# Loading two weight matrices in fp32 on SyncE's queue and casting them on POOL, in a kernel of channel attention and gelu

## The chip, the cores and the metric

The kernel runs on one core of a Trainium2 chip. The metric is the time of one execution in device microseconds (us). The granted clock is the share of the full TensorE clock in the profile's record. Engines are called by the names of the profile: PE (TensorE), DVE (VectorE), ACT (ScalarE), POOL (GpSimd), SP (SyncE). SP's loads stand in the profile as the hardware queue, POOL's as the software queue. A load lands when its last byte has arrived; a casting load turns fp32 into bf16 on its way.

## The reference

```python
B, N, C = 4, 6080, 256                                    # q, k, v: fp32
qn = q / (norm(q, axis=1) + 1e-06); kn = k / (norm(k, axis=1) + 1e-06)
s  = kn.transpose(0, 2, 1) @ qn / tau                     # 256 x 256 for each batch
a  = softmax(s)                                           # over the last axis
x  = (v @ a).reshape(24320, 256)
h  = x @ w_in                                             # w_in 256 x 2048
g  = gelu_tanh(h)
out = g @ w_out                                           # w_out 2048 x 256
```

## The kernel before

The kernel multiplies the attention of each batch into w_in (`aw`), so that the main loop has two stages for each block of 512 tokens: hp = v·aw with gelu on ACT, and yp = g·w_out. For the first batch, q and k come in fp32 on SP's queue in eight chunks, into a ring of four staging buffers, and the products q·k and the column sums must be complete before anything else can start; this opening takes some 41 us. The next batches' attention is woven into the main loop.

The parts that matter here: the four staging buffers, the small copy that holds POOL back until chunk 5 has landed, and the casting loads of the weights on POOL's queue.

```python
stage = ctx.enter_context(tc.tile_pool(name="stage", bufs=4))
# ... for each chunk n of the first batch: cast on DVE, square on ACT, products on PE, then
        for x in ((2, 3) if n == 0 else (4, 5) if n == 1 else (n + 4,)):
            stage_chunk(x)                                # next loads on SP's queue
        if n == n_chunks - 3:
            nc.gpsimd.tensor_copy(gate[:, 0:1], st[1][0:1, 0, 0:1])
# ... v block 0 in fp32 on SP's queue, then
    for c0, c1 in ((0, 1024), (1024, D)):
        nc.gpsimd.dma_start(out=win_bf[:, :, c0:c1], in_=win_v[:, :, c0:c1])
    load_v(1)
    for half in range(2):
        nc.gpsimd.dma_start(out=wout_bf[:, half * 8 : half * 8 + 8, :],
                            in_=wout_v[:, half * 8 : half * 8 + 8, :])
    load_v(2)
# ... norms, Gs, its transposes T, eT = exp(T); then the first products with w_in (first_aw),
#     aw scaled on DVE and ACT, and the main loop:
    #   hp  L584: lhsT=aw,  rhs=vT       yp  L510: lhsT=g, rhs=wout_bf[:, fc, :]
    #   in the first block, yp of fc 0-3, 4-7 and 8-11 follow hp groups 5, 6 and 7
```

Of the kernel before, what the change touches and what calls it, by code (L numbers as in the profile page):

```python
# [8 lines left out]
FP32 = mybir.dt.float32  # L9
# [9 lines left out]
def kernel(  # L19
# [10 lines left out]
    nc = tc.nc  # L30
    B, N, C = q.shape
    D = moe_w_in.shape[1]
# [12 lines left out]
    stage = ctx.enter_context(tc.tile_pool(name="stage", bufs=4))  # L45
# [19 lines left out]
    SMAX = 6  # L65
# [22 lines left out]
    def slots_of(chunk, rest=REM):  # L88
        _, size, rem = chunk
        return [(s, 128) for s in range(size)] + ([(size, rest)] if rem else [])  # L90
# [9 lines left out]
    def halves(pool, tag, dtype, size, most=SMAX):  # L100

        tiles = [pool.tile([128, 2, most, 256], dtype, tag=tag, name=tag)
                 for _ in range(1 if size <= most else 2)]
        if len(tiles) == 1:
            return [tiles[0][:, x] for x in range(2)], tiles[0]
        return [t.rearrange("p a b c -> p (a b) c") for t in tiles], None

    def stage_chunk(n):
        if n < len(first_chunks):
            _, size, rem = first_chunks[n]  # L110
            if n < SHARED:
                st, whole = halves(stage, "st", FP32, size)
            else:

                _, size, rem = first_chunks[n - 2]
                whole = staged[n - 2][1][:, :, size + rem :, :]
                st = [whole[:, x] for x in range(2)]
                rem = False

            if rem:  # L120
                nc.gpsimd.memset(whole[:, :, size, :], 0.0)
            load_chunk((nc.sync, nc.scalar if n < 1 else nc.sync), st, 0, first_chunks[n], 2)
            staged.append((st, whole))
# [16 lines left out]
    gate = const.tile([1, 8], FP32)  # L140
# [3 lines left out]
    win_bf = const.tile([128, 2, D], BF16)  # L144
    wout_bf = const.tile([128, FC, 256], BF16)
    win_v = moe_w_in.rearrange("(c p) d -> p c d", p=128)
    wout_v = moe_w_out.rearrange("(t p) d -> p t d", p=128)

    def keep_clock(n, pool=pH, tag="h"):

        for _ in range(n):
            idle = pool.tile([128, 2, 512] if pool is pH else [128, 512], FP32, tag=tag, name="idle")
            nc.tensor.matmul(idle[:, 0, :] if pool is pH else idle, lhsT=filler[:, 0:128], rhs=filler, start=True, stop=True)

    def gram(G, qk, s, rows, first, last):
        for ic in range(2):
            nc.tensor.matmul(  # L157
                G[:, ic, :],
                lhsT=qk[1][:rows, s, ic * 128 : ic * 128 + 128],
                rhs=qk[0][:rows, s, :],  # L160
                start=first and ic == 0,
                stop=last,
                skip_group_check=True,
            )
# [66 lines left out]
    n_chunks = len(first_chunks)  # L231
    seen, summed = 0, 0

    def sums_of(parts, last):
        nonlocal summed
        for m, x in enumerate(parts):
            col_sums(cols, x, ones_bf[: x[0].shape[0], :], summed == 0, last and m == len(parts) - 1)
            summed += 1

    def pairs_of(n, sqb):  # L240

        size = first_chunks[n][1]
        h = size // 2
        pair, whole = halves(prp, "pair", BF16, h, SMAX // 2)
        for x in range(2):
            nc.vector.tensor_add(pair[x][:, 0:h], sqb[x][:, 0:h], sqb[x][:, h : 2 * h])
        parts = [[y[:, s, :] for y in pair] for s in range(h)]
        if size % 2:
            parts.append([y[:, size - 1, :] for y in sqb])
        if first_chunks[n][2]:  # L250
            parts.append([y[:, size, :] for y in sqb])
        sums_of(parts, False)

    waiting = None
    for n, ch in enumerate(first_chunks):
        st, whole = staged[n]
        size = ch[1]
        qkb, qk_whole = halves(qkp, "qk", BF16, size)
        sqb, sq_whole = halves(sqp, "sq", BF16, size)
        hi = size + ch[2]  # L260
        if whole is None:
            todo = list(zip(qkb, sqb, st))
        else:
            todo = [[y[:, :, 0:hi] for y in (qk_whole, sq_whole, whole)]]
        for to, sq, x in todo:
            nc.vector.tensor_copy(to, x)  # L266
            if n != n_chunks - 2:
                nc.scalar.activation(sq, x, AF.Square)  # L268
        if n == n_chunks - 2:
            nc.scalar.activation(sqb[1][:, 0:hi], st[1][:, 0:hi], AF.Square)  # L270
            nc.vector.tensor_mul(sqb[0][:, 0:hi], qkb[0][:, 0:hi], qkb[0][:, 0:hi])
        keep_clock(fillers[n])
        for s, rows in slots_of(ch, 128):
            gram(G, qkb, s, rows, seen == 0, seen == n_all - 1)
            seen += 1
        if waiting is not None:
            pairs_of(*waiting)
            waiting = None
        if n < 2:
            pairs_of(n, sqb)  # L280
        elif n < TAIL:
            waiting = (n, sqb)
        else:
            sums_of([[y[:rows, s, :] for y in sqb] for s, rows in slots_of(ch, 128)], n == n_chunks - 1)

        for x in ((2, 3) if n == 0 else (4, 5) if n == 1 else (n + 4,)):
            stage_chunk(x)
        if n == n_chunks - 3:
            nc.gpsimd.tensor_copy(gate[:, 0:1], st[1][0:1, 0, 0:1])

    v0 = stage.tile([128, 2, SMAX, 256], FP32, tag="st", name="v0")
    v0 = v0.rearrange("p a b c -> p (a b) c")[:, 0:4, :]
# [2 lines left out]
    def v_parts(nb):  # L295
        blk = nb % n_blocks
        cols = min(BLK, N - blk * BLK)
        return (nb // n_blocks) * N + blk * BLK, cols // 128, cols % 128
# [4 lines left out]
    def load_v(nb):  # L303
        if nb >= B * n_blocks:
            return
        r0, n, rest = v_parts(nb)
        t = vin.tile([128, 4, 256], BF16, tag="v", name="vb")
        nc.gpsimd.dma_start(  # L308
            out=t[:, 0:n, :],
            in_=v_rows[r0 : r0 + n * 128, :].rearrange("(p s) c -> p s c", s=n))  # L310
        if rest:
            nc.gpsimd.dma_start(out=t[:rest, n, :], in_=v_rows[r0 + n * 128 : r0 + n * 128 + rest, :])
        v_of[nb] = t
# [27 lines left out]
            load_chunk((nc.gpsimd, nc.gpsimd), views, b, later_chunks[n])  # L341
            loaded_of[b, n] = views, t

    for c0, c1 in ((0, 1024), (1024, D)):
        nc.gpsimd.dma_start(out=win_bf[:, :, c0:c1], in_=win_v[:, :, c0:c1])
    load_v(1)
    for half in range(2):
        nc.gpsimd.dma_start(out=wout_bf[:, half * 8 : half * 8 + 8, :],
                            in_=wout_v[:, half * 8 : half * 8 + 8, :])
    load_v(2)  # L350


    r = smx.tile([128, 4], FP32, tag="r", name="r")
# [5 lines left out]
    for cc in range(2):  # L359
        p = pH.tile([128, 2, 512], FP32, tag="h", name="vps")[:, 0, :]  # L360
# [183 lines left out]
    for b in range(B):  # L544
# [5 lines left out]
        for blk in range(n_blocks):  # L550
# [27 lines left out]
            for i in range(NP):  # L578
# [12 lines left out]
                if before is not None:  # L591
                    n = -(-len(before["todo"]) // (NP - i))
                elif i >= NP - 3:

                    n = 4
                else:
                    n = 0
# [58 lines left out]
```

## Time and profile before

| | value |
|---|---|
| time | 756.42 us, median of 3 (756.24 to 757.38) |
| span in the profile | 754.2 us, granted clock 1.0 |
| PE busy | 733.3 us, 97% |
| first gelu matmul (hp) | 41.05 us |
| first half of w_in landed | 39.61 us |

The two lines that say most are from the view of waits of PE (engine and line, what it waited for; total us, times, longest). The view has four rows. Apart from PE's wait for the first casts of q and k (15.6 us, 14.4 of them before its first instruction), the first row here is the only one above half a microsecond, and the only one that a load of weights causes:

```profile
PE ps L384 <- DMA win_bf<-in_moe_w_in_dram: 1.3, 1, 1.3
PE T L195 <- DVE Gs L187: 0.3, 1, 0.3
```

The profile's time at which a matmul group starts is what I compare below. Since the opening takes a few tenths of a microsecond more or less from one execution to the next, I count from the transposes of v block 0, which stand right after the last product of the opening: they start at 35.86, the first gelu matmul follows 5.19 us later, and the second block's first gelu matmul (52.32) 16.46 us later.

### The profile page before, as it was taken

How to read it: one execution, taken by the hardware profiler on the slowest of the kernel's cores; microseconds unless marked ns; L12 is line 12 of the kernel's file. 1: busy time of each engine (PE TensorE's matmuls, PEld its weight loads, DVE VectorE, ACT ScalarE, POOL GpSimd, SP SyncE). 2: the span in 40 equal slices, each digit the busy share in tenths (PEclk: the TensorE clock that was granted, in tenths of full speed). 3: DMA queues.
4: the chain of work that ended last, by engine and by line, in shares of the span. 5: the costliest groups of instructions: out<-in, count | busy, mean ns of one | idle time of the engine just before them, and what ended most of it. 6: DMA issues, size and time to landing. Idle time of an engine off the chain costs nothing.

```text
span 754.2 us, 12371 instructions
## 1 busy us (share of the span) xinstructions
PE 733.3 (97%) x5262; PEld 503.5 (67%) x5262; DVE 277.5 (37%) x485; ACT 420.3 (56%) x411; POOL 75.6 (10%) x150
## 2 busy tenths in 40 slices
PE   2999999999999999999999999999999999999998
PEld 1656666776666666776666666766767666666666
DVE  3733556454401546554521265555441011011011
ACT  4875555555456555555555555555546655555552
POOL 1311111101012102101001102010101000000000
PEclk9999999999999999999999999999999999999999
DMA  9999685615147685813435776661513543322111
GB/s 368 346 190 156 103 150 137 118 43 83 48 93 143 114 161 108 162 52 60 99 57 118 140 117 121 148 133 46 83 43 80 96 95 74 69 74 54 41 56 57
DMA packets 79639, 83.59 MB, mean 111 GB/s; under 512 B 55392, under 2 KB 59104, under 8 KB 79072
## 3 DMA queue, kind: packets, MB, share of 16 engines
q0 software_dynamic: 17104, 32.97, 27.4%
q1 hardware_dynamic: 62176, 48.20, 23.8%
q10 hardware_dynamic: 304, 1.64, 0.5%
q8 instruction: 41, 0.67, 0.4%
q14 instruction: 14, 0.11, 0.0%
HBM read 78.91 MB, written 24.90 MB: 138 GB/s over the span
## 4 chain that ended last, share of the span: by engine, by line
PE 94%; DMA 4%; ACT 1%; issue 0%; DVE 0%; SPq 0%; POOL 0%; DVEq 0%
PE yp L510 44%; PE hp L584 44%; PE G L157 4%; PE ps L217 2%; ACT sq L268 1%; DMA st<-in_q_dram 1%; DMA st<-in_k_dram 1%; DMA win_bf<-in_moe_w_in_dram 1%; PE cols L169 0%; PE yp L615 0%; PE T L195 0%; DVE aw L404 0%; PE vps L422 0%; PE ps L384 0%; PE rs L204 0%
## 5 line engine op out<-in xcount | busy, mean ns | idle before, releaser
L588 ACT ACTIVATE g<-hp 128x1024 bf16<-128x1024 f32 (+1 forms) x384 | 389.8, 1015 | 308.2 <-PE hp L584 308.2
L510 PE MATMUL yp<-wout_bf,g 128*128 128x256 bf16 x3024 | 392.0, 273 | 0.0
L584 PE MATMUL hp<-vT,aw 128*128 128x512 bf16 (+1 forms) x1536 | 390.8, 377 | 0.2 <-DVE aw L404 0.2
L510 PEld LDWEIGHTS <-g 128*128 128x128 bf16 x3024 | 295.9, 98 | 113.4
L584 PEld LDWEIGHTS <-aw 128*128 128x128 bf16 x1536 | 149.9, 98 | 104.7 <-issue 0.6
L527 DVE COPY ysb<-yp 128x512 f32<-128x512 f32 (+1 forms) x95 | 64.9, 683 | 402.5 <-PE yp L510 402.5
L451 DVE TENSOR_TENSOR acc<-acc,sq 128x512 f32<-128x512 f32 (+1 forms) x141 | 97.5, 692 | 4.8
L450 DVE TENSOR_TENSOR sq<-qkb 128x512 bf16<-128x512 bf16 (+1 forms) x141 | 58.7, 417 | 0.0
L157 PE MATMUL G<-qkb 128*128 128x256 bf16 (+1 forms) x288 | 55.0, 273 | 0.0
L308 POOL DMA_DIRECT2D vb<-in_v_dram x47 | 25.8, 551 | 76.6 <-DMA vT<-vb 64.3
L226 DVE TENSOR_SCALAR aw<-ps,rsinv 128x512 bf16<-128x512 f32 x30 | 22.4, 749 | 27.1 <-PE ps L217 26.7
L157 PEld LDWEIGHTS <-qkb 128*128 128x128 bf16 (+1 forms) x288 | 27.9, 98 | 3.8 <-issue 0.6
L333 POOL CAST gate<-g 1x1 f32<-1x1 bf16 x24 | 5.9, 244 | 237.3 <-ACT g L588 237.3
L157 PE MATMUL G<-qk 128*128 128x256 bf16 x96 | 13.7, 301 | 15.6 <-DVE qk L266 15.6
L268 ACT ACTIVATE sq<-st 128x3072 bf16<-128x3072 f32 (+2 forms) x9 | 21.1, 2379 | 11.2 <-DMA st<-in_q_dram 8.2
L157 PEld LDWEIGHTS <-qk 128*128 128x128 bf16 x96 | 9.9, 108 | 19.0 <-DVE qk L266 16.6
L266 DVE CAST qk<-st 128x3072 bf16<-128x3072 f32 (+2 forms) x10 | 14.2, 1437 | 13.2 <-DMA st<-in_q_dram 10.0
L217 PE MATMUL ps<-win_bf,eT 128*128 128x512 bf16 x60 | 17.7, 379 | 0.0
L461 POOL TENSOR_TENSOR r<-r,half 128x4 f32<-128x4 f32 x3 | 3.1, 1043 | 113.8 <-DVE r L460 113.8
L81 POOL DMA_DIRECT2D qkb<-in_q_dram x24 | 12.8, 535 | 6.8 <-issue 4.7
L81 POOL DMA_DIRECT2D qkb<-in_k_dram x24 | 12.9, 538 | 0.0
L567 POOL COPY g<-gr 128x1024 bf16<-128x1024 bf16 x2 | 2.1, 1036 | 105.1 <-PE yp L510 105.1
(69 smaller groups left out, 100.7 us busy)
## 6 DMA issues: line engine op xcount, KB each, us to landing
out_dram<-ysb SPq DMA_DIRECT2D x44, 512.0 KB, 2.9
vb<-in_v_dram POOLq DMA_DIRECT2D x43, 256.0 KB, 6.8
qkb<-in_q_dram POOLq DMA_DIRECT2D x21, 384.0 KB, 4.7
qkb<-in_k_dram POOLq DMA_DIRECT2D x21, 384.0 KB, 6.5
st<-in_q_dram SPq DMA_DIRECT2D x2, 1536.0 KB, 11.8
vT<-vb SPq DMA_TRANSPOSE x184, 3.0
st<-in_k_dram ACTq DMA_DIRECT2D x1, 1536.0 KB, 10.3
st<-in_k_dram SPq DMA_DIRECT2D x1, 1536.0 KB, 16.7
```

Of the source, the lines that this page charges most:

```text
L81: engines[x].dma_start(out=dst[x][:, 0:size, :], in_=src[b, s0 * 128 : (s0 + size) * 128, :].rearrange("(p s) c -> p s c", s=size))
L157: nc.tensor.matmul(G[:, ic, :], lhsT=qk[1][:rows, s, ic * 128 : ic * 128 + 128], rhs=qk[0][:rows, s, :], start=first and ic == 0, stop=las ...
L217: nc.tensor.matmul(ps, lhsT=eT[:, jc, ic * 128 : ic * 128 + 128], rhs=win_bf[:, jc, fs * 512 : fs * 512 + 512], start=jc == 0, stop=jc == 1)
L226: nc.vector.tensor_scalar_mul(dst, ps, scale)
L268: nc.scalar.activation(sq, x, AF.Square)
L308: nc.gpsimd.dma_start(out=t[:, 0:n, :], in_=v_rows[r0 : r0 + n * 128, :].rearrange("(p s) c -> p s c", s=n))
L450: nc.vector.tensor_mul(sq[:rows], flat, flat)
L451: nc.vector.tensor_add(acc[:rows], acc[:rows], sq[:rows])
L510: nc.tensor.matmul(yp[:rows, at, :], lhsT=g[:, fc, s * 128 : s * 128 + rows], rhs=wout_bf[:, fc, :], start=fc == 0, stop=fc == FC - 1)
L527: nc.vector.tensor_copy(ysb[:, s0 : s + 1, :], yp[:, 0 : s + 1 - s0, :])
L584: nc.tensor.matmul(hp[:, j, :cols], lhsT=aw[:, cc, fc * 128 : fc * 128 + 128], rhs=vT[:, cc, :cols], start=cc == 0, stop=cc == 1)
L588: nc.scalar.activation(g[:, 2 * i : 2 * i + 2, :cols], hp[:, :, :cols], AF.Gelu_apprx_tanh)
```

## The change

The intent: PE should not wait for w_in. The weights join the order of SP's queue, directly behind v block 0, in fp32 (the loads on SP's queue do not cast), w_in in quarters so that the first piece is small; POOL casts each piece as it lands, and issues the loads of v blocks 1 and 2 between the casts. The wait on chunk 5 is dropped.

```diff
-        if n == n_chunks - 3:
-            nc.gpsimd.tensor_copy(gate[:, 0:1], st[1][0:1, 0, 0:1])
...
-    for c0, c1 in ((0, 1024), (1024, D)):
-        nc.gpsimd.dma_start(out=win_bf[:, :, c0:c1], in_=win_v[:, :, c0:c1])
-    load_v(1)
+    def flat_stage(n):
+        w = stage.tile([128, 2, SMAX, 256], FP32, tag="st", name="wst")
+        return w.rearrange("p a b c -> p (a b c)")[:, 0:2048].rearrange("p (c d) -> p c d", c=n)
+
     for half in range(2):
-        nc.gpsimd.dma_start(out=wout_bf[:, half * 8 : half * 8 + 8, :],
-                            in_=wout_v[:, half * 8 : half * 8 + 8, :])
-    load_v(2)
+        w = flat_stage(2)
+        for x in range(2):
+            c0 = half * 1024 + x * 512
+            nc.sync.dma_start(out=w[:, :, x * 512 : x * 512 + 512], in_=win_v[:, :, c0 : c0 + 512])
+            nc.gpsimd.tensor_copy(win_bf[:, :, c0 : c0 + 512], w[:, :, x * 512 : x * 512 + 512])
+        load_v(1 + half)
+    for half in range(2):
+        w = flat_stage(8)
+        nc.sync.dma_start(out=w, in_=wout_v[:, half * 8 : half * 8 + 8, :])
+        nc.gpsimd.tensor_copy(wout_bf[:, half * 8 : half * 8 + 8, :], w)
```

## The prediction

> **What bounds the kernel now.** I read the page first: engine sums, DMA queues and the chain that ended last.
>
> ```profile
> span 754.2 us, 12371 instructions
> PE 733.3 (97%) x5262; PEld 503.5 (67%) x5262; DVE 277.5 (37%) x485; ACT 420.3 (56%) x411; POOL 75.6 (10%) x150
> ...
> q0 software_dynamic: 17104, 32.97, 27.4%
> q1 hardware_dynamic: 62176, 48.20, 23.8%
> ...
> HBM read 78.91 MB, written 24.90 MB: 138 GB/s over the span
> ...
> PE 94%; DMA 4%; ACT 1%; issue 0%; DVE 0%; SPq 0%; POOL 0%; DVEq 0%
> ```
>
> PE is busy 97% of the span and makes up 94% of the last chain. Of the 21 us in which PE is idle (754.2 - 733.3), 14.4 pass before its first instruction, and the rest lies in the first 41 us. The change touches only the end of that opening: how two weight matrices get on chip. It can win only what is still a wait there.
>
> A second reading of these lines: the casting loads on the software queue count their written bf16 bytes. Doubled they are 65.94 MB; with the 12.97 MB of first-batch q, k and v block 0 that the hardware queue reads (my sum of their sizes) that makes exactly the 78.91 MB of HBM reads. So "200 GB/s" in a stretch of casting loads is 400 GB/s read: the cast in the DMA costs no read rate, and the change does not reduce the bytes to be read.
>
> Next, the chain that ended last, in order of time (start, length, what), cut to the first 80 us:
>
> ```profile
> 22.04 9.61 DMA st<-in_k_dram
> ...
> 31.71 0.12 POOL gate L289
> 31.83 7.78 DMA win_bf<-in_moe_w_in_dram
> 39.61 0.14 issue
> 39.74 0.38 PE ps L384 x2
> ...
> 40.24 0.18 DVE rsinv L210
> ...
> 41.05 1.04 PE hp L584 x4
> ```
>
> POOL waits until chunk 5 has landed (31.71), issues w_in, and its first half lands at 39.61; PE goes on at 39.74, the first gelu matmul runs at 41.05, and from there the chain is PE alone. How much of the 7.78 us is really a loss is in the timeline (start, length, engine, line, what, idle before and its releaser):
>
> ```profile
> 38.23 0.84 ACT L374 ACTIVATE eT<-T,r 128x256 bf16<-128x256 f32 x2 [0.50 <-PE T L195]
> 38.95 0.60 ACT L375 ACTIVATE vT<-vps 128x512 bf16<-128x512 f32 x1
> ...
> 39.74 0.38 PE L384 MATMUL ps<-win_bf,eT 128*128 128x256 bf16 x2 [1.34 <-DMA win_bf<-in_moe_w_in_dram]
> ...
> 51.88 0.60 PE L510 MATMUL yp<-wout_bf,g 128*128 128x256 bf16 x4
> ```
>
> PE sat 1.34 us, but eT, the other operand, has its first half only at about 38.65 (38.23 plus half of 0.84). So w_in was late by about one microsecond: that is the whole prize, 0.13% of 756.
>
> **What the Trainium skill says.** "DMA: Bandwidth & Descriptors", section "Issuing engines are not separate DMA queues": loads from any issuing engine run on the same 16 engines and interleave. The trace agrees: 407 GB/s from 20 to 30 us on SyncE's queue, about 200 written (400 read) from 42 to 50 us on POOL's. Moving the weights to SyncE's queue buys order, not rate. The same page, "SWDGE vs HWDGE vs iDMA", says that a cast during DMA can only be issued from GpSimd; hence the explicit casts. "GPSIMD Engine Reference", section "Elementwise — side-by-side cycle accounting": a simple body runs at 1.03 cycles an element, which at the 1.2 GHz of "Trainium Kernel Development and Optimization" ("NeuronCore Architecture") is 0.86 ns. The trace agrees for bf16 copies: 128x1024 takes 1036 ns and a one-element copy 179, so 0.84 ns an element; the only fp32-to-bf16 cast on POOL (128x128, 291 ns) gives 0.87. "SBUF — State Buffer", "Who interferes with whom": POOL and VectorE block each other only when VectorE runs a two-port mode or reads two SBUF inputs. Between 37 and 51 us VectorE reads PSUM almost throughout, so I expect undisturbed casts; no run of before has such a cast to show it.
>
> **The change, part by part.**
>
> Removed: POOL's wait on chunk 5 and four casting loads of weights. The data of the first batch hardly gets faster: the hardware queue moved 372 to 388 GB/s until 34 us, nearly its full rate, although w_in was already issued.
>
> Added, loads: four quarters of w_in (512 KB each, fp32) and two halves of w_out (1 MB each) in SyncE's order behind v block 0. They wait for staging buffers and for completion slots eight DMAs back. By the program's waits and the trace: quarter 0 goes when chunk 3's square is done (28.5) and chunk 4's k has landed (29.15); quarter 1 when chunk 5's q has landed (about 30.5); quarters 2 and 3 when chunk 6's square has ended (34.2); w_out's first half after chunk 7's square (35.5), its second after PE's transposes of v block 0 (36.9). The queue holds earlier bytes until each of these, so it doesn't run dry. Block 0 of v was issued at 27.0 and took 8.6, landing at 35.6. A quarter is 524,288 bytes; at 407 GB/s that is 1.29 us. Landings: quarters at 36.9, 38.2, 39.5, 40.8.
>
> Added, casts (estimates from the POOL rows above): 0.18 + 1024 x 0.84 ns = 1.04 us for a quarter, 0.18 + 2048 x 0.84 = 1.90 us for half of w_out. POOL in its order: quarter 0 done at 38.0, quarter 1 at 39.3, load of v 1 issued (0.57 us) by 39.9, quarters 2 and 3 done at 40.9 and 42.0, load of v 2 by 42.6, then w_out as it lands.
>
> On the path: PE needs quarter 0 at about 38.7 (eT plus some 0.07 of semaphore), and has it at 38.0. So the wait on w_in vanishes and eT takes its place. First product at 38.75, its partner at 38.97; the row sums need eT's second half (39.07) and the inverse starts near 39.4 in place of 40.24. From there the old spacing holds, so the gelu stage starts about 0.85 us sooner, at 40.2. Quarter 1 (done 39.3) is wanted at 41.1, quarter 2 (40.9) at 42.8, quarter 3 (42.0) at 45.4: all in time.
>
> Then w_out. After v block 0 the engines must move 4.19 MB of weights and 1.05 MB of v blocks 1 and 2 before its second half is complete: 5.24 MB at 407 GB/s is 12.9 us, landing near 48.5 and cast at 50.4. The first half lands near 44.6 and is cast at 46.5; PE wants it at 48.0 (48.84 less 0.85). The second half is wanted by the third group of output matmuls, 51.88 less 0.85 = 51.0. Margins: 1.5 and 0.6 us. In before the second half landed 14.1 us after its issue at 35.6, at 49.7, with 2.2 us to spare: the cast eats most of that.
>
> Later effects: v 3 and the next batch's first q, k chunk are issued after the last cast, near 51 rather than 48; they take about 8 us and are first used at 66.8. Hidden. From 42 us on PE is full either way, so a gain at the start moves the end one for one. Sum: -0.85 us if the margins hold.
>
> **The rivals.**
>
> A, the second half of w_out comes late. For it: the margin is 0.6 us, the rate is assumed to hold for w_out's 1 KB rows, and a cast at two thirds of my rate would add nearly a microsecond. PE runs in order, so each microsecond late is lost in full. Against: the halves are issued early and nothing but v 1 and v 2 competes. If a fifth more time is needed for the 5.24 MB, 2.6 us, the stall is 2 us and the total is 1.1 us up: 757.5.
>
> B, quarter 0 is no earlier. If fp32 casts take twice as long, or the load lands two microseconds later, PE waits for POOL rather than DMA, with nothing won: 756.4, or a little more as the rest comes late too.
>
> C, more is won: without the software queue beside it, chunks 6 and 7 and v block 0 land sooner, gram ends sooner, and everything behind follows. For it: VectorE and ScalarE wait for chunks there. Against: the rate was nearly full. It would add at most some 0.4 us: 755.1.
>
> **Range and chances.** Full gain gives 755.6. I give rival A a third, with a mean stall of about 0.8, hence 0.25 on average: 755.8. The three runs of before span 1.1 us themselves. Range 754.8 to 757.2. Two per cent is 15 us; the part of the span that the change touches is shorter than that, and PE's wait there is 1.3. Faster 0.5%, same 98.5%, slower 1%.
>
> **What would show each step.** In the timeline of after: the first product with w_in near 38.8, with PE released by eT rather than a load (if POOL's cast releases it, B); casts of about 1.04 and 1.90 us on POOL; the first gelu matmul at 40.2; no wait of the output matmuls for POOL near 50 us (if there is one, its length is rival A's loss). PE's busy time should stay at 733, as its instructions are the same. I am wrong if the gelu stage starts at 41 or later, if PE idles over 1 us between 42 and 55 us, or if the time leaves the range.

## The result, and the profile after

The changed kernel took 756.04, 756.45 and 755.67 us; a fourth run, 910.63 us at a granted clock of 0.81, is left out. The kernel before had a median of 756.5 beside it (four executions). The ratio of after to before is 0.9992, 95% interval 0.9972 to 1.0012: the same. (Ratios here are the mean time of one kernel's fast runs over the mean of the other's in the same rounds, so they are not quite the ratio of the medians.)

The page of after, in the lines that answer to those of before (engine sums, the DMA queues, the chain that ended last):

```profile
span 754.3 us, 12301 instructions
PE 729.5 (97%) x5175; PEld 503.9 (67%) x5262; DVE 277.6 (37%) x485; ACT 420.3 (56%) x411; POOL 79.3 (11%) x151
...
q0 software_dynamic: 14480, 30.87, 25.3%
q1 hardware_dynamic: 65344, 52.39, 24.7%
...
HBM read 78.91 MB, written 24.90 MB: 138 GB/s over the span
...
PE 92%; DMA 5%; ACT 1%; issue 1%; POOL 1%; SPq 0%; DVE 0%; ACTq 0%; POOLq 0%
```

HBM reads are unchanged, 78.91 MB: bytes moved from the software to the hardware queue and nothing was saved, as the prediction read. (PE's sum of 729.5 can't be held against the forecast of 733: 87 of its 5262 matmul records are missing from this trace; the weight loads are all there.) What is new is POOL in the last chain. In order of time, cut to the first 80 us:

```profile
35.66 10.22 DMA wst<-in_moe_w_out_dram
...
45.93 1.90 POOL wout_bf L356
...
50.01 1.91 POOL wout_bf L356
...
51.96 0.60 PE yp L516 x4
```

Before, the chain went through w_in at 39.61; now it goes through the second half of w_out, which is cast from 50.01 to 51.92. The timeline shows both sides of the account (start, length, engine, line, what, idle before and its releaser):

```profile
38.80 0.39 PE L390 MATMUL ps<-win_bf,eT 128*128 128x256 bf16 x2 [0.35 <-ACT eT L380]
...
40.25 1.04 PE L590 MATMUL hp<-vT,aw 128*128 128x512 bf16 x4 [0.18 <-DVE aw L410]
...
50.22 1.03 PE L590 MATMUL hp<-vT,aw 128*128 128x512 bf16 x4
51.96 0.60 PE L516 MATMUL yp<-wout_bf,g 128*128 128x256 bf16 x4 [0.72 <-POOL wout_bf L356]
```

The gain is there: the first product with w_in is released by eT, and the first gelu matmul comes at 40.25 in place of 41.05, 4.26 us after the transposes of v block 0 in place of 5.19. Then it is handed back: the four matmuls at 50.22 are followed 0.86 us later elsewhere in the chain, so the third output group should start at 51.08; it starts at 51.96, when POOL's cast has ended. That is 0.88 us. The second block starts at 52.40 against 52.32 before, and from there the two kernels run in step (at 508 us in both chains, the same product ends with the same 0.08 us between them).

### The profile page after: what moved, and what is told of

It reads as the page before. It is cut to its first block, busy times and chain, and to the rows that moved or that the text cites. A ratio compares the mean times of both kernels' runs of the same rounds, so it can differ in the third digit from the quotient of the medians.

```text
span 754.3 us, 12301 instructions
## 1 busy us (share of the span) xinstructions
PE 729.5 (97%) x5175; PEld 503.9 (67%) x5262; DVE 277.6 (37%) x485; ACT 420.3 (56%) x411; POOL 79.3 (11%) x151
## 3 DMA queue, kind: packets, MB, share of 16 engines
HBM read 78.91 MB, written 24.90 MB: 138 GB/s over the span
## 4 chain that ended last, share of the span: by engine, by line
PE 92%; DMA 5%; ACT 1%; issue 1%; POOL 1%; SPq 0%; DVE 0%; ACTq 0%; POOLq 0%
PE yp L516 44%; PE hp L590 42%; PE G L157 4%; DMA st<-in_k_dram 2%; DMA st<-in_q_dram 1%; DMA wst<-in_moe_w_out_dram 1%; PE ps L217 1%; ACT sq L268 1%; POOL wout_bf L356 1%; PE cols L169 0%; PE yp L621 0%; PE T L195 0%; ACT g L594 0%; SPq L81 0%; DVE ysb L624 0%
## 5 line engine op out<-in xcount | busy, mean ns | idle before, releaser
L590 PE MATMUL hp<-vT,aw 128*128 128x512 bf16 (+1 forms) x1457 | 384.4, 377 | 3.9 <-DVE aw L410 0.2
L81 POOL DMA_DIRECT2D qkb<-in_q_dram x24 | 12.9, 536 | 6.4 <-issue 4.6
L81 POOL DMA_DIRECT2D qkb<-in_k_dram x24 | 12.9, 538 | 0.0
```

The costliest lines, as they stand in the source:

```text
L81: engines[x].dma_start(out=dst[x][:, 0:size, :], in_=src[b, s0 * 128 : (s0 + size) * 128, :].rearrange("(p s) c -> p s c", s=size))
L590: nc.tensor.matmul(hp[:, j, :cols], lhsT=aw[:, cc, fc * 128 : fc * 128 + 128], rhs=vT[:, cc, :cols], start=cc == 0, stop=cc == 1)
```

## The experiments

My theory: the opening wins 0.9 us, and PE's wait for the cast of w_out's second half gives 0.9 back; the rest of the program has no slack and no effect. The rivals: the equality is chance; the wait is of another kind; or PE's later work would have taken the delay up anyway. In the table, "to gelu" and "to block 2" are the distances from the start of v block 0's transposes to the first gelu matmul of the first and of the second block, in the profile of each run.

| run | to gelu | to block 2 | median time | ratio to before, 95% interval |
|---|---|---|---|---|
| before | 5.19 | 16.46 | 756.42 | |
| before again (h1) | 5.28 | 16.55 | 756.54 | 1.0008 (0.9994 to 1.0022) |
| after | 4.26 | 16.41 | 756.04 | 0.9992 (0.9972 to 1.0012) |
| after again (e1) | 4.26 | 16.57 | 756.07 | 0.9991 (0.9977 to 1.0005) |
| casts split (e2) | 4.26 | 15.52 | 755.70 | 0.9984 (0.9972 to 0.9997) |
| w_out in quarters (e3) | 4.26 | 15.52 | 755.50 | 0.9986 (0.9972 to 1.0000) |
| the same again (g3) | 4.26 | 15.52 | 755.57 | 0.9987 (0.9975 to 1.0000) |
| last cast twice (e4) | 4.26 | 17.94 | 758.50 | 1.0023 (1.0010 to 1.0036) |
| only w_in the new way (f1) | 4.78 | 17.92 | 762.12 | 1.0059 (1.0035 to 1.0084) |
| only w_out the new way (g2) | 5.56 | 17.79 | 759.36 | 1.0035 (1.0021 to 1.0049) |
| v block 2 last (f2) | 4.26 | 15.52 | 763.65 | 1.0083 (1.0069 to 1.0097) |
| w_in's first load small (g1) | 4.39 | 15.65 | 756.07 | 0.9989 (0.9975 to 1.0002) |

The ratios mix executions at full clock with some at a mean clock of 0.997 or 0.998, of which the kernel before had more (see h1). Of the round with e1 to e4, the executions at 0.999 or more alone have these means: before 756.39 (five), e1 756.14 (five), e2 755.41 (four), e3 755.79 (five), e4 757.81 (two). So some of the 0.9991 of e1 is clock; the differences of e2 and e4 from before, -1.0 and +1.4 us, are near those of "to block 2", -0.94 and +1.48. f3 and f4, with wrong results on purpose, are not in the table: one execution each, 755.08 and 756.60 us, of unknown state.

### e1: the changed kernel again

No edit.

> The changed kernel again, more rounds beside the kernel before. My theory (the opening wins 0.80 us, PE's wait for the cast of w_out's second half gives 0.88 back): a ratio within 0.1% of 1, in the trace the first gelu matmul near 40.2 and PE idle 0.7 to 1 us before the third group of output matmuls near 51. If the equal times were only chance and the opening's gain survives (rival), the ratio would be about 0.999 and that wait would be absent in this run.

The ratio was 0.9991 and the trace repeated the account: first gelu matmul at 40.03, cast from 49.95 for 1.89 us, and PE idle for it 0.83 us. So the near equality is no chance: the gain and the wait are both there again.

### e2: each half of w_out cast in two pieces

```diff
-        nc.gpsimd.tensor_copy(wout_bf[:, half * 8 : half * 8 + 8, :], w)
+        for x in (0, 4):
+            nc.gpsimd.tensor_copy(wout_bf[:, half * 8 + x : half * 8 + x + 4, :], w[:, x : x + 4, :])
```

> Each half of w_out is loaded as before but cast as two pieces of 4 rows, so that PE waits for 1.04 us of cast after the landing (49.99) instead of 1.90. My theory: the wait near 51 falls from 0.9 to about 0.05 us, the span shrinks by 0.8 us (753.5), ratio near 0.999. Rival (the load's landing itself, not the cast, sets it, or PE's start is held by something else then): the span stays at 754.2 or so.

The loads are unchanged; PE now waits for the cast of four rows of the half in place of eight. The wait is gone from the view of waits, "to block 2" falls from 16.41 to 15.52, by 0.89 us, and the ratio is 0.9984. The span was 753.9 where I expected 753.5: this execution's opening was itself 0.5 us longer (v's transposes at 36.53). A smaller piece to cast was enough to remove the loss.

### e3 and g3: w_out loaded and cast in quarters

```diff
-        nc.sync.dma_start(out=w, in_=wout_v[:, half * 8 : half * 8 + 8, :])
-        nc.gpsimd.tensor_copy(wout_bf[:, half * 8 : half * 8 + 8, :], w)
+        for x in (0, 4):
+            f0 = half * 8 + x
+            nc.sync.dma_start(out=w[:, x : x + 4, :], in_=wout_v[:, f0 : f0 + 4, :])
+            nc.gpsimd.tensor_copy(wout_bf[:, f0 : f0 + 4, :], w[:, x : x + 4, :])
```

> w_out is loaded and cast in four pieces of 512 KB. My theory: the third piece lands near 48 and is cast by 49.5, PE never waits for it and the whole gain of the opening, 0.8 us, stays: span 753.4, time about 755.6 against 756.4. If the loss is of another kind, nothing is won: span 754.3.

> w_out in four pieces again, beside the run with w_in in quarters on POOL's queue: no wait of PE for w_out, about 0.9 us under the kernel before where the granted clock is full. Where the clock falls in the opening, both gain nothing, as eT is later than w_in in either kernel.

Both profiles show no wait for w_out: its third quarter is cast from 49.22 (48.49 in the second run), and PE takes it at 51.38 and 51.44 without a pause. Landing "near 48" was a microsecond too hopeful in the first. The distance to block 2 is 15.52 in both, the same as in e2: this is the floor once neither weight is waited for. The times, 755.50 and 755.57, with both intervals reaching just to 1.0000, are, with e2's 755.70, the best of the kernels with right results; in each, the whole of the opening's gain is kept. The remark on lower clocks in the expectation is not settled by these runs (see h1).

### e4: the last cast done twice

```diff
-        nc.gpsimd.tensor_copy(wout_bf[:, half * 8 : half * 8 + 8, :], w)
+        for _ in range(1 + half):
+            nc.gpsimd.tensor_copy(wout_bf[:, half * 8 : half * 8 + 8, :], w)
```

> The second half of w_out is cast twice in a row: 1.90 us more on POOL, nothing else. My theory: PE runs in order and is full afterwards, so the wait grows from 0.9 to 2.8 us and the time by 1.9 us (758.3, ratio about 1.0025). If PE's later work has slack that takes such delays up (rival), the time grows by clearly less than 1.9 us.

PE's wait in the timeline:

```profile
49.62 3.85 POOL L357 CAST wout_bf<-wst 128x2048 bf16<-128x2048 f32 x2 [3.34 <-DMA wst<-in_moe_w_out_dram]
...
53.52 0.60 PE L517 MATMUL yp<-wout_bf,g 128*128 128x256 bf16 x4 [2.26 <-POOL wout_bf L357]
```

PE starts 0.05 us after the second cast. The load landed 0.4 us earlier this time (49.62 with the opening at 36.02, against 50.01 at 35.99), so "to block 2" rose by 17.94 - 16.41 = 1.53 us for 1.95 us of added cast, and the span by 1.6 over e1's (755.8 against 754.2). The delay is passed on in full; nothing later takes it up.

### f1: w_in alone the new way

```diff
-        w = flat_stage(8)
-        nc.sync.dma_start(out=w, in_=wout_v[:, half * 8 : half * 8 + 8, :])
-        nc.gpsimd.tensor_copy(wout_bf[:, half * 8 : half * 8 + 8, :], w)
+        nc.gpsimd.dma_start(out=wout_bf[:, half * 8 : half * 8 + 8, :],
+                            in_=wout_v[:, half * 8 : half * 8 + 8, :])
```

> Only w_in goes the new way; w_out is loaded by casting DMAs on POOL's queue again, issued after the four casts of w_in. My theory: the gain of the opening (4.26 in place of 5.19 us from the transposes of v block 0 to the first gelu matmul) stays and no cast follows w_out's landing; issued near 42.5, its second half lands at about 49 to 50.5, before PE wants it at 51.1: no wait, ratio near 0.9985. Rival: what made w_out late is POOL's place in the order rather than the cast, so a casting DMA issued only at 42.5 lands after 51 and PE waits as long or longer: ratio 1 or above.

My expectation failed and the rival held. POOL works in order, so w_out's loads were issued only at 43.11, after w_in's last cast; between 43 and 44 us the DMA engines moved 20 GB/s, with work left that nobody had asked for. PE then waited twice for w_out, 0.67 and 0.87 us. Six executions lie between 757.6 and 764.3; the profiled one, 758.6, is one of the two fast ones. What costs the four at 761.7 and above is not seen in a profile. (The load issued last, at 44.88, is that of v block 3; v block 2 went at 42.59, ahead of w_out, so it was not late as in f2 below. The cause stays open.)

This profile shows one thing more, by accident. The opening ran late here, at a granted clock of 0.81 from 18 to 22 us and 0.53 from 22 to 24, and so POOL's first cast met DVE's work on the norms, a step of the path to eT:

```profile
36.91 1.04 POOL L351 CAST win_bf<-wst 128x1024 bf16<-128x1024 f32 x1 [22.18 <-DMA wst<-in_moe_w_in_dram]
...
37.28 0.69 DVE L180 TENSOR_SCALAR r<-r 128x4 f32<-128x4 f32 x1 [2.27 <-ACT r L359]
```

The addition over 128x4 elements takes 0.17 us in after (at 36.38, before the cast at 37.18); here it took 0.69 and ended at 37.97, 0.02 us after the cast. In f4, also late, it took 0.49 and ended with the cast as well. That agrees with the lock between POOL and DVE that the Trainium skill describes in "SBUF — State Buffer", "Who interferes with whom". The additions are longer by 0.52 and 0.32 us, which is just what "to gelu" is longer in these two runs, 4.78 and 4.58 in place of 4.26.

### f2: v block 2 loaded after w_out's casts

```diff
-        load_v(1 + half)
+        if half == 0:
+            load_v(1)
...
         nc.gpsimd.tensor_copy(wout_bf[:, half * 8 : half * 8 + 8, :], w)
+    load_v(2)
```

> The load of v block 2 is issued after both casts of w_out, everything else as in the changed kernel. If the transfers share one pool of bandwidth, w_out's second half is 0.52 MB, 1.3 us, ahead: it lands at about 48.7, is cast by 50.6 and PE doesn't wait near 51; ratio near 0.9985. If w_out is late for a reason of its own queue (its 1 KB rows, the descriptors) and not for the shared engines, it lands near 50 as before and the wait of 0.9 us stays.

The part that was expected came: w_out's second half was cast from 49.63, which counted from the transposes of v block 0 is 12.93 us, against 14.02 in after: 1.1 us earlier for 0.52 MB that no longer went ahead. (The same loads in e1, e2 and e4 give 14.18, 13.88 and 13.60, so the gain is between 0.7 and 1.3 us.) PE didn't wait near 51. This is what one pool of bandwidth for both queues would give. But the kernel became 7 us slower. The timeline of PE:

```profile
71.36 1.86 PE L592 MATMUL hp<-vT,aw 128*128 128x512 bf16 x4 [6.39 <-DMA vT<-vb]
```

The load of v block 2, issued at 51.47, let SP start its transposes only at 55.34; the last transpose of the block landed at 71.2, and PE had nothing else to do. In after they start at 49.00. The idle time then cost PE its clock: it was granted 0.50 from 71 to 75 us. That agrees with "TensorE: Matmul & The Clock Gate" of the Trainium skill, section "HAM oscillation — how this bites in real kernels", which warns of idle gaps above about 3.4 us; here the gap was 6.39. So "v blocks 1 and 2 between the casts" is not decoration: this place in the order is worth 7 us.

### f3 and f4: what slows the queue

Why did w_out land at 50.0 and not at 48.5? The windows of after (stretch in us; busy time of PE, PEld, DVE, ACT and POOL; granted clock; DMA share; GB/s) show a slow stretch, between 38 and 42 us with the hardware queue alone at work:

```profile
34.00:36.00 2.00, 2.00 (x44) 1.77 (x42) 1.10 (x2) 1.39 (x2) 0.00 (x0) 1.00 1.05 388
36.00:38.00 2.00, 1.57 (x18) 1.29 (x16) 1.48 (x5) 1.66 (x3) 0.82 (x1) 1.00 1.09 343
38.00:40.00 2.00, 1.65 (x15) 0.85 (x13) 0.80 (x3) 1.63 (x4) 1.73 (x3) 1.00 0.94 277
40.00:42.00 2.00, 1.82 (x10) 0.81 (x10) 1.22 (x4) 1.97 (x4) 1.38 (x3) 1.00 1.00 310
```

Two kernels with wrong results on purpose (the check of outputs says so; each is one look) change only which rows of a weight go to which partition, and with it the length of the contiguous runs. f3 reads w_out in runs of 8 KB in place of 1 KB:

```diff
+    wout_long = moe_w_out.rearrange("(p t) d -> p t d", p=128)
...
-        nc.sync.dma_start(out=w, in_=wout_v[:, half * 8 : half * 8 + 8, :])
+        nc.sync.dma_start(out=w, in_=wout_long[:, half * 8 : half * 8 + 8, :])
```

> Wrong result on purpose: w_out is read with 8 KB contiguous rows for each partition in place of 1 KB rows; the bytes are the same. The queue moved only about 271 GB/s from 37.5 to 40 us and 310 from 40 to 42, against 388 before 36. If the short rows slow the queue, w_out's second half lands about 1.3 us earlier, near 48.7, and PE doesn't wait. If the slow stretch belongs to w_in or the moment, the landing stays near 50 with the stretch from 37.5 to 40 as slow as before.

```profile
36.00:38.00 2.00, 1.78 (x16) 1.27 (x14) 1.57 (x5) 1.66 (x3) 0.92 (x1) 1.00 1.02 352
38.00:40.00 2.00, 1.64 (x15) 0.79 (x12) 0.80 (x3) 1.72 (x4) 1.72 (x3) 1.00 0.99 338
40.00:42.00 2.00, 1.83 (x9) 0.89 (x10) 1.22 (x4) 1.97 (x4) 1.39 (x3) 1.00 1.01 418
```

The rate from 40 to 42 us rises from 310 to 418 GB/s (277 to 329 in the runs with the loads of after: after, e1, e2 and e4), and the second half's cast starts at 48.03 in place of 50.01. PE waits for nothing; "to block 2" is 15.52, the floor. So most of the late landing comes from w_out's short rows. f4 reads each quarter of w_in as 4 KB in one run in place of two runs of 2 KB:

```diff
+    win_flat = moe_w_in.rearrange("(p c) d -> p (c d)", c=2)
...
-            nc.sync.dma_start(out=w[:, :, x * 512 : x * 512 + 512], in_=win_v[:, :, c0 : c0 + 512])
+            nc.sync.dma_start(out=piece, in_=win_flat[:, 2 * c0 : 2 * c0 + 1024])
```

> Wrong result on purpose: each quarter of w_in is read as 4 KB contiguous for each partition in place of two 2 KB pieces of rows 8 KB apart; bytes and order are the same. If w_in's pattern makes the slow stretch, the rate from 37.5 to 40 us rises from 271 to about 390 GB/s and all later landings are about 0.8 us earlier. If not, nothing moves.

From 38 to 40 us the rate was 373 in place of 277 GB/s (277 to 310 in after, e1, e2 and e4), so the pattern of w_in had a part in the slow stretch. But w_out's second half still landed only just before 49.69, 0.3 us earlier than in after: not the 0.8 that I expected, and inside the 49.62 to 50.41 of after, e1, e2 and e4. (The opening was late in this run: v block 0 landed at 35.6, but PE began its transposes only at 37.12. So its PE waits say nothing, and w_out's second half, which waits for these transposes, was issued at 38.2 in place of 37.1. Only the rates are a fair look.) What part of the stretch from 36 to 40 us in f3 is w_in's pattern and what the overlap with w_out, these two looks do not separate.

### g1: the kernel before with its first load cut in two

```diff
-    for c0, c1 in ((0, 1024), (1024, D)):
+    for c0, c1 in ((0, 512), (512, 1024), (1024, D)):
```

> The kernel before with one edit: its casting load of w_in's first half is cut into two quarters, all still on POOL's queue. If the gain of the opening is only one of order (PE needs a quarter of w_in first, not a half, and needs no other queue or cast for it), the first quarter lands near 38, PE is released by eT, the first gelu matmul comes 4.3 us after the transposes of v block 0 begin in place of 5.2, and since w_out's landing at 49.7 doesn't move and no cast follows, the whole 0.9 us stays: about 755.5. If the software queue's start is what made the first half late (rival), the quarter lands no earlier than 39 and at most 0.3 us is won.

This is one line in the kernel before, with casting loads and no staging. The profiled execution had a late opening (granted clock 0.50 from 22 to 24 us), so eT itself came late, and that PE waits for eT and not for w_in proves less than it would otherwise. But the landing settles it: the loads of w_in were issued from 31.89 on, and the first quarter landed 4.9 us later, at 36.8 (view of tile win_bf), sooner than the 38 that I expected and well before the 38.65 at which eT has its first half in before. So the rival, that the software queue's start is what made the first half late, falls. The times support it: its executions at a clock of 0.999 or more took 755.72, 756.07 and 755.28, mean 755.69; those of the kernel before in the same rounds 755.96, 756.80, 755.67, 756.98 and 756.92, mean 756.47; g3's 755.57, 755.25, 756.37 and 755.03, mean 755.56. The interval of its ratio, 0.9975 to 1.0002, still touches 1. No run drops POOL's wait on chunk 5 alone; g1 keeps it and has the gain nevertheless.

### g2: w_out alone the new way

```diff
+    load_v(2)
     for half in range(2):
-        nc.gpsimd.dma_start(out=wout_bf[:, half * 8 : half * 8 + 8, :],
-                            in_=wout_v[:, half * 8 : half * 8 + 8, :])
-    load_v(2)
+        w = stage.tile([128, 2, SMAX, 256], FP32, tag="st", name="wst")
+        # ... viewed as [128, 8, 256]
+        nc.sync.dma_start(out=w, in_=wout_v[:, half * 8 : half * 8 + 8, :])
+        nc.gpsimd.tensor_copy(wout_bf[:, half * 8 : half * 8 + 8, :], w)
```

> The other half of the change alone: w_in by casting loads on POOL behind chunk 5 as before, w_out in fp32 on SyncE's queue (in the next two staging buffers, so its first half goes before chunk 7 is done) and cast on POOL. My theory: nothing is won in the opening, and w_out's transfers now run beside w_in's, so w_in lands later than 39.6 and PE's wait for it grows beyond 1.3 us; 757 to 758.5. Rival, that the loss lies in w_out's cast alone: the opening stays as before and only a wait near 52 appears.

The load of v block 2 goes ahead of w_out's here. It took 759.36, rather above what I had expected. PE waited 1.48 us for w_in, until 41.09, although eT was late as well (clock 0.50 from 22 to 24 us here too); so w_in landed some 1.4 us later than in before, as expected from two queues on the same engines, and there was no wait near 52. After this wait the granted clock fell again, to 0.50 from 42 to 44 us, which I had not foreseen and which accounts for part of the loss: four gelu matmuls took 1.91 us in place of 1.04. Of the 2.9 us by which this span (757.1) is longer than that of before, 1.3 are the later opening (transposes at 37.16), 0.4 the later gelu stage and 1.0 the longer way from the first group of gelu matmuls to the second (2.71 us in place of 1.74).

### h1: the kernel before again

No edit.

> The kernel before, unchanged. About half of its executions so far have a mean clock of 0.997 to 0.998 and take 757.6 to 758.4 us, the others 1.0 and 755.7 to 757.0; those of the changed kernel were nearly all of the second kind. If this profile falls on one of the first kind it shows where the clock falls: near 22 us in the opening, as in three profiles of other variants, or after PE's wait for w_in near 41, as in the run with w_out alone, where the first gelu matmuls ran at half clock. If it falls on the second kind, it only repeats the profile of before, with PE's wait of 1.3 us for w_in.

The profile fell on an execution at clock 1.0 and repeated before: PE waits 1.43 us for w_in, "to gelu" 5.28, "to block 2" 16.55. Where the executions at a lower clock lose their time in the kernel before stays open. They were 19 of the 46 executions of the kernel before in the rounds of these experiments (mean clock 0.997 or 0.998), and none of the 8 fast executions of the changed kernel; whether the change makes them rarer, the runs do not tell.

## Why the prediction was right or wrong

- **PE bounds the kernel; only the opening can be won.** Right. From 52 us on, before and after run in step.
- **w_in comes in time; eT takes its place; the gelu stage at 40.2.** Right: 40.25. The gain that I put at 0.85 us is 0.80 by the clock of the two traces and 0.93 counted from v's transposes.
- **Rivals B and C.** Neither came: eT, not POOL, released the first product with w_in (B), and v's transposes began at 35.99 against 35.86, so the first batch's data was no sooner there (C).
- **Casts of 1.04 and 1.90 us on POOL.** Right to the hundredth: 1040 and 1897 ns. The rate was taken from a bf16 copy, and the fp32 source made no difference. The casts were undisturbed, as I expected; the reverse, which I hadn't asked, shows in f1 and f4, where a cast held up DVE.
- **The order of the loads.** The quarters of w_in began to be cast at 37.18, 38.49, 40.46 and 41.81, where 36.9, 38.2, 39.5 and 40.8 had been forecast for their landing. Late by up to 1.0 us, and still in time for PE.
- **The margin of w_out.** Here a term was mis-sized, and with it the verdict "-0.85 us if the margins hold". The step reads "5.24 MB at 407 GB/s is 12.9 us, landing near 48.5 and cast at 50.4". It landed near 50.0 and was cast at 51.92. The rate of 407 came from long rows; w_in's and w_out's short ones went at 277 to 343 from 36 to 42 us. A margin of +0.6 became -0.88, and rival A, to which I gave a third, came true with a stall of about the mean that I had named, 0.8. Of its reasons, the 1 KB rows are what f3 shows; the cast rate was not to blame.
- **The total.** 756.04 against 755.8, well inside 754.8 to 757.2. The range was right because both outcomes lay in it, and that was luck rather than a sign of the mechanism: it could not have told the full gain from none. The central number leaned on the gain that was given back.
- **Later effects hidden.** Right for this kernel, but with less room than the words suggest: f2, which delays v block 2 by 8.7 us, costs 7 us. I had looked at v 3 and at the next q and k, and not asked how long the transposes of v block 2 take.
- **Two readings of the trace of before were wrong, without effect.** The idle time of PE outside the opening is not nil: its last matmul ends at 750.75, so 3.5 of the 21 us lie at the end of the span. And v 3 was not issued near 48 but at 37.03, right behind v 2; the change put it off to 51.85, by 15 us and not 3; PE did not wait for it.

## What to carry to other kernels

When a transfer is moved forward, follow every piece behind it to its consumer, with the rate of its own row length: here 0.9 us were won at one wait and given back at another some eleven microseconds later, behind a cast. Cut what is cast on arrival to the size that the consumer takes, so that the last landing is followed by a short cast. And look first for the smaller edit: cutting the first casting load in two in the kernel before, one line, got a time near that of the whole change mended.

## What the Trainium skill lacked or had wrong

- "DMA: Bandwidth & Descriptors", section "Specifications", gives 512 B as the smallest transfer for line rate. On the hardware queue here, with 1 KB rows of w_out, 310 GB/s were moved from 40 to 42 us and 357 from 42 to 44; with 8 KB rows, 418 and 390 (f3, one look).
- "GPSIMD Engine Reference" has no duration of a cast from fp32 to bf16: 1040 ns for 1024 elements a partition and 1897 for 2048, thus 0.84 ns an element.
- "SBUF — State Buffer" is right on the lock between POOL and DVE, and says that the one that comes second is blocked for the whole instruction of the other. It has no time for a short DVE instruction behind a cast on POOL: an addition of four elements a partition took 0.69 us in place of 0.17 and ended with the cast (f1).
- "TensorE: Matmul & The Clock Gate" speaks of idle gaps above about 3.4 us; that frequent short idling can do the same it says too, but not how much. In g2 the clock fell to 0.50 after a wait of 1.48 us, with PE busy for 1.19 of the 3 us from 38 to 41; so a thin stretch was enough in that execution. In before PE was busy for 1.36 of the 3 us from 37 to 40, and the clock stayed at 1.0, as it did after the like wait in h1; these runs give no threshold.
